# A gated mix of two attentions on one core: the first 512 tokens turned by TensorE instead of by DMA

## The chip, the cores and the metric

The kernel runs on one core of a Trainium2 chip. The metric is the device time of one execution in microseconds (us); for each kernel several executions are timed and the median is taken. One further execution is recorded by the hardware profiler, and all views below are of that one.

The core's engines are named as in the profile: PE is TensorE (matrix products), PEld its weight loads, DVE is VectorE, ACT is ScalarE, POOL is GpSimd, SP the engine that issues most DMAs.

## The reference

One input x of 2048 tokens by 512 goes through two attention blocks, each with 32 heads of 16, and the results are mixed by a gate per token:

```python
x = A_x
g = sigmoid((x * gate_w).sum(-1, keepdims=True))
# A: softmax attention
q, k, v = split(x @ A_wqkv)                     # 32 heads of 16
p = softmax(q @ k.T / 4)                        # 2048 x 2048 for each head
a = (p @ v) @ A_wo
# B: linear attention with a learned feature map
q, k, v = split(x @ B_wqkv)
phi = lambda t: concat(softmax(t @ w_phi), softmax(-(t @ w_phi)))
kv, z = phi(k).T @ v, phi(k).sum(tokens)
b = (phi(q) @ kv / (phi(q) @ z + 1e-6)) @ B_wo
return g * a + (1 - g) * b
```

Block A has 32 x 2048 x 2048 = 134 million exponentials; they are the bulk of the work.

## The kernel before, in words

**Tiles.** x is kept turned, as `xT` (features on the partitions, 4 chunks of 128, tokens along the row). From it `kT`, `qT` and `V` are projected. A *unit* is a score tile of one head: 128 keys by 512 queries, one bank of PSUM. Four units (four heads) of one key tile make a *pack*; a *head group* is 16 packs (all key tiles of four heads, for one chunk of 512 queries); there are 32 head groups and 512 packs.

**Two ways to take an exponential.** Most packs go to ScalarE: `_qk` writes three or two banks of scores (a ring of five banks), `_exp` reads them in one ACTIVATE and writes bf16 to slots of `ET` (30 slots), and `_pv` multiplies by V. The packs named in `AWAY` (a bit mask of up to five packs for each head group) go to VectorE instead: `_vector_bits` turns scores into bf16 bit patterns with one multiply-add, and `_vector_terms` (VectorE and GpSimd) makes two shifted copies whose sum corrects the approximation; TensorE adds the three terms. Block B's steps, the projections of later heads, and the stores are fitted in between.

**Order.** All work is declared as operations with an engine, an estimated cost, dependencies and a priority (a due time in packs). A planner (`Plan.order`) simulates five engines and writes an in-order queue for each; in the same sweep it hands out the free PSUM banks. Each operation belongs to a tag such as `p37` or `b103`, and the table `SHIFT` moves the priorities of a tag by a number found by search. The queues are fixed when the kernel is built.

**The start.** `_loads` queues on SP two transposing DMAs for the first 512 tokens (256 each, lines 529 to 531 and 1390), then three for the other tokens (512 each), then weights. ACT's own queue carries the first 128 columns of the key, query and value weights (`WA`, line 525). `_warm` (line 635) runs nine matmuls on ones from the start. `_proj_k0` and `_proj_q0` then project keys and queries of the first head group in halves of 256 tokens, each needing one of the two DMAs. The queries are copied out of PSUM twice, each time times a mask that keeps every other head (line 719, VectorE, four copies in all). The first scores need both halves of the queries and the first half of the keys.

Lines that the prediction names: 525 (loads of `WA`), 572 (ones for the warm-up), 639 (warm-up), 646 (projections in four column tiles), 662 (key projection in halves), 678 (its copy), 713 and 719 (query projection and its copies), 736 (value projection), 940 (`_vector_bits`), 1022 (scores), 1070 (exponentials), 1135 (products with V), 1238 (a copy of turned weights of block B out of PSUM), 1390 (transposing DMAs), 1496 (the last copies of the output by ScalarE), 1501 (stores).

Of the kernel before, what the change touches and what calls it, by code (L numbers as in the profile page):

```python
# [6 lines left out]
ACT = mybir.ActivationFunctionType  # L7
# [3 lines left out]
P = 128  # L11
# [375 lines left out]
class _Kernel:  # L387
# [122 lines left out]
    def _loads(self):  # L510
# [18 lines left out]
        for half in range(2):  # L529
            load_x(0, QCH // 2 * half, QCH // 2 * (half + 1), 4.1)  # L530
            self.b_x0[half].writers = self.b_xT[0].writers[half:]
# [64 lines left out]

    def _projections(self):
# [11 lines left out]
        self._warm(9)  # L609
# [25 lines left out]
    def _warm(self, n):  # L635

        def run(e):
            for _ in range(n):
                ins = e.matmul(self.ps[:, 4, :], self.warm[:, 0:P], self.warm, start=True, stop=True)
            return ins  # L640
        self.plan.op("PE", run, 0.427 * n, reads=[self.b_warm], name="warm", prio=-99)
# [63 lines left out]
    def _proj_q0(self, half, bank):  # L705
# [12 lines left out]
        for side in range(2):  # L718
            o = op("DVE", lambda e, side=side: e.tensor_scalar(
                self.qT[:, side, at], self._bank(job)[:, 0:QCH // 2], self.mask[:, side:side + 1], None, op0=ALU.mult),  # L720
                self.c_dve(256), reads=[self.b_mask], deps=[m], name="qproj_ev", prio=-40 + 70 * side,
                release=pool if side else None)
            self.b_qT[side].writers.append(o)
# [23 lines left out]
    def _gate(self):  # L747
# [44 lines left out]
    AWAY = (22, 27, 28, 19, 26, 15, 29, 27, 27, 15, 15, 30, 31, 13, 15, 27, 15, 23, 31, 27, 27, 31, 31, 31, 26, 31, 25, 31, 30, 15, 19, 31)  # L792

    SHIFT = (
# [752 lines left out]
```

## Time and profile before

| | us |
|---|---|
| median of 3 runs (lowest, highest) | 743.38 (743.01, 743.54) |
| the profiled execution, its own time | 743.37 |
| its span, first to last instruction | 741.6 |
| ACT busy in it | 727.0 |
| DVE busy in it | 693.9 |
| PE busy in it | 710.9 |

The granted TensorE clock is 1.00 over the whole span. How to read the views: a row of instructions gives its start and length in us, the engine, the line of the kernel, output and inputs by tile name, and in brackets how long the engine stood idle before and what ended that. A row of groups gives the number of instructions, their busy time, the mean length of one in ns, and the idle time before them. A row of stretches gives, after the stretch and its length, the busy time of PE, PEld, DVE, ACT and POOL with their numbers of instructions, then the granted clock, the share of the DMA engines and GB/s. A row such as "272/273/321" has the shortest, median and longest duration in ns. Lengths of instructions on one engine overlap, since the engines are pipelined.

### The profile page before, as it was taken

What the parts mean: (1) busy time and instruction counts of PE and PEld (TensorE: products, weight loads), DVE (VectorE), ACT (ScalarE), POOL (GpSimd) and SP (SyncE); (2) the same over time, 40 slices, a digit from 0 to 9 for tenths busy, and PEclk for the clock granted to TensorE, in tenths of its full rate; (3) what the DMA queues carried; (4) which work ended last, traced back from release to release, by engine and by line L of the source; (5) the groups of instructions that cost most, each with busy time, mean ns of one, the idle gap of its engine ahead of it and who ended that gap; (6) DMA issues with size and microseconds to landing.
All of it is one profiled execution on the core that took longest, in us unless ns stands there. A gap on an engine that the chain in (4) does not pass through costs nothing.

```text
span 741.6 us, 19810 instructions
## 1 busy us (share of the span) xinstructions
PE 710.9 (96%) x8580; PEld 232.8 (31%) x8599; DVE 693.9 (94%) x1097; ACT 727.0 (98%) x635; POOL 279.7 (38%) x277
## 2 busy tenths in 40 slices
PE   8999999999999999999998999999999999999998
PEld 4334333333232322322222223322323233322322
DVE  5889989988999999999999999999999999999996
ACT  6999999999999999999999999999999999999996
POOL 4631331423434335232434344245342433325342
PEclk9999999999999999999999999999999999999999
DMA  9400000000000010000101301131211320231110
GB/s 201 142 12 14 12 2 13 13 4 13 14 9 11 3 22 8 9 9 8 16 8 20 55 14 32 30 76 13 31 23 30 51 44 8 39 81 20 23 23 30
DMA packets 90040, 21.96 MB, mean 30 GB/s; under 512 B 82912, under 2 KB 89440, under 8 KB 89952
## 3 DMA queue, kind: packets, MB, share of 16 engines
q1 hardware_dynamic: 88224, 20.17, 14.5%
q8 instruction: 67, 1.10, 0.6%
q10 hardware_dynamic: 1728, 0.52, 0.3%
q14 instruction: 21, 0.17, 0.1%
HBM read 4.21 MB, written 2.10 MB: 9 GB/s over the span
## 4 chain that ended last, share of the span: by engine, by line
ACT 89%; PE 6%; DVE 2%; DMA 1%; SPq 0%; issue 0%; DVEq 0%
ACT ET L1070 85%; ACT bq L1308 4%; PE ps L1022 2%; PE ps L1135 2%; PE ps L646 2%; DVE va L940 1%; DVE vp L962 1%; DMA xT<-in_A_x_dram 1%; DMA WT<-nb 1%; PE ps L736 0%; DVE bq L1279 0%; DVE nb L1420 0%; SPq L1390 0%; ACT xT L1496 0%; DVE rb L1418 0%
## 5 line engine op out<-in xcount | busy, mean ns | idle before, releaser
L1070 ACT ACTIVATE ET<-ps 128x1536 bf16<-128x1536 f32 x615 | 699.8, 1372 | 5.2 <-PE ps L1022 4.9
L977 POOL TENSOR_SCALAR vp<-va 128x1024 uint16<-128x1024 uint16 x260 | 271.8, 1045 | 450.4 <-DVE va L940 137.7
L940 DVE TENSOR_SCALAR va<-ps 128x512 uint16<-128x512 f32 x512 | 335.2, 684 | 25.1 <-PE ps L1022 22.0
L1022 PE MATMUL ps<-qT,kT 32*128 32x512 bf16 x2048 | 311.6, 384 | 20.3 <-ACT ET L1070 15.9
L1022 PEld LDWEIGHTS ps<-qT,kT 32*128 32x128 bf16 x2048 | 81.0, 91 | 265.9 <-ACT ET L1070 165.3
L962 DVE TENSOR_SCALAR vp<-va 128x4096 uint16<-128x4096 uint16 (+1 forms) x143 | 159.4, 1123 | 0.6 <-PE ps L1135 0.4
L1135 PE MATMUL ps<-ET,V 128*32 128x512 bf16 x1536 | 148.4, 385 | 1.4 <-DVE T L1156 1.3
L1135 PE MATMUL ps<-vp,vc 128*32 128x512 bf16 x1024 | 93.3, 384 | 0.3 <-DVE vp L962 0.3
L646 PE MATMUL ps<-WB,xT 128*32 128x512 bf16 x768 | 57.9, 382 | 0.0
L1135 PEld LDWEIGHTS ps<-ET,V 128*32 128x32 bf16 x1536 | 39.3, 95 | 57.1 <-issue 40.7
L1142 PE MATMUL ps<-kT,zero 128*32 128x512 bf16 x552 | 50.1, 385 | 0.4 <-ACT ET L1070 0.3
L1135 PE MATMUL ps<-va,V 128*32 128x512 bf16 x512 | 50.2, 385 | 0.0
L1135 PE MATMUL ps<-vp,V 128*32 128x512 bf16 x512 | 47.1, 384 | 0.7 <-DVE vp L962 0.7
L646 PE MATMUL ps<-xT,WA 128*32 128x512 bf16 x480 | 36.1, 382 | 0.3 <-DVE va L940 0.3
L1135 PEld LDWEIGHTS ps<-vp,vc 128*32 128x32 bf16 x1024 | 24.4, 95 | 35.9 <-issue 24.9
L1308 ACT ACTIVATE bq<-bq 128x2048 bf16<-128x2048 bf16 x16 | 32.7, 2046 | 0.0
L1156 DVE STREAM_TRANSPOSE T<-ps 128x512 f32<-128x512 f32 x32 | 22.7, 709 | 1.7 <-PE ps L1135 1.7
L646 PE MATMUL ps<-WoA,onTA 128*32 128x512 bf16 x256 | 23.2, 383 | 0.0
L646 PE MATMUL ps<-WoB,WT 128*32 128x512 bf16 x256 | 23.0, 383 | 0.0
L1279 DVE CAST bq<-ps 128x512 bf16<-128x512 f32 x32 | 21.8, 683 | 1.1 <-PE ps L646 1.1
L646 PEld LDWEIGHTS ps<-WB,xT 128*32 128x32 bf16 x768 | 15.6, 95 | 19.0 <-issue 11.2
L1135 PEld LDWEIGHTS ps<-va,V 128*32 128x32 bf16 x512 | 13.3, 95 | 20.4 <-issue 16.6
(86 smaller groups left out, 357.9 us busy)
## 6 DMA issues: line engine op xcount, KB each, us to landing
turned<-T SPq DMA_DIRECT2D x240, 8.0 KB, 1.8
qT<-qs SPq DMA_DIRECT2D x120, 16.0 KB, 1.8
WB<-in_B_wqkv_dram SPq DMA_DIRECT2D x1, 1536.0 KB, 6.9
out_dram<-WB SPq DMA_DIRECT2D x12, 128.0 KB, 1.9
WA<-in_A_wqkv_dram SPq DMA_DIRECT2D x3, 384.0 KB, 6.1
WoA<-in_A_wo_dram SPq DMA_DIRECT2D x1, 512.0 KB, 7.9
WoB<-in_B_wo_dram SPq DMA_DIRECT2D x1, 512.0 KB, 8.8
WA<-in_A_wqkv_dram ACTq DMA_DIRECT2D x3, 128.0 KB, 3.6
```

What stands on the lines that cost most here:

```text
L646: ins = e.matmul(out[32 * g:32 * g + 32], lhs[:, 32 * g:32 * g + 32], rhs, start=start, stop=stop, tile_position=(0, 32 * g), skip_group_c ...
L940: parts.append(op("DVE", lambda e, j=j, job=job: e.tensor_scalar(self.va[:, pair, side, j, :], self._bank(job), SCALE * LOG2E * 128.0, (12 ...
L962: self.plan.op("DVE", lambda e, k=k, shift=shift: e.tensor_scalar(flat(self.vp[:, k]), flat(self.va[:, pair]), float(shift), None, op0=ALU ...
L977: o = self.plan.op("POOL", lambda e, flat=flat: e.tensor_scalar(flat[0], flat[1], 1.0, float(shift), op0=ALU.mult, op1=ALU.add), 0.08 + n ...
L1022: return e.matmul(out, self.kT[32 * i:32 * i + 32, cp, kt * TOK:(kt + 1) * TOK], self.qT[32 * i:32 * i + 32, s, :], start=True, stop=True, ...
L1070: o = plan.op("ACT", lambda e: e.activation(self.ET[:, a % NS:a % NS + n, :], self.ps[:, self._ring(a):self._ring(a) + n, :], ACT.Exp, sca ...
L1135: ins = e.matmul(self._bank(ot)[32 * i:32 * i + 32, :], V[:, v0:v0 + 32], tile(), start=(kt == 0), stop=(kt == self.NT - 1), tile_position ...
L1142: ins = e.matmul(self._bank(ot)[32 * i:32 * i + 32, :], self.zero[:], self.kT[:, 0, 0:QCH], start=False, stop=False, tile_position=(0, 32 ...
L1156: self.turned_out = op("DVE", lambda e: e.transpose(T1[:, side].rearrange("p b s -> p (b s)"), src()), 0.635, deps=last, writes=[b_T1[side ...
L1279: [lambda e, b, k=k: e.tensor_copy(bq[:, k].rearrange("p (g s v) -> p g s v", g=8, s=2)[:, :, 0, :], b.rearrange("p (g v) -> p g v", g=8))],
L1308: op("ACT", lambda e, side=side: e.activation(sides[side], sides[side], ACT.Exp, scale=1.0 - 2 * side), self.c_act(2048) + 0.04, reads=[bu ...
```

## The change

The first 512 tokens are loaded by four plain DMAs of 128 tokens each, as they lie, into slots 20 to 23 of `ET` (not yet used at that time). TensorE turns each with four transposes into one PSUM bank; the bank is copied to `xT` by VectorE for the first and third set of tokens, by ScalarE for the second and fourth. The nine warm-up matmuls become four, with one more after the second and one after the fourth set. Of the four masked copies of queries, one (second half, first mask) moves to ScalarE. `AWAY` and the whole table `SHIFT` are replaced; the table has 128 bits set before and after.

```diff
-        for half in range(2):
-            load_x(0, QCH // 2 * half, QCH // 2 * (half + 1), 4.1)
-            self.b_x0[half].writers = self.b_xT[0].writers[half:]
+        self.x0 = [self.dma("SP", f"x{t}", lambda e, t=t: e.dma_start(
+            self.ET[:, 20 + t], self.x2d[TOK * t:TOK * t + TOK, :]), cost=0.45, prio=-60 + t, lat=2.3) for t in range(4)]
...
+    def _first_tokens(self):
+
+        op = self.plan.op
+        for t in range(4):
+            job, pool = self._job(t if t < 2 else None)
+
+            def turn(e, t=t, job=job):
+                for c in range(4):
+                    ins = e.transpose(self._bank(job).bitcast(BF16)[:, P * c:P * c + P], self.ET[:, 20 + t, P * c:P * c + P], self.iden[:])
+                return ins
+            m = op("PE", turn, 4 * self.c_pe(128), reads=[self.b_iden], deps=[self.x0[t]], name="xtr", prio=-90 + t,
+                   acquire=pool)
+            if t % 2:
+                self._warm(1, [m])
+            out = self.xT[:, :, TOK * t:TOK * t + TOK]
+            src = lambda job=job: self._bank(job).bitcast(BF16)[:, 0:QCH].rearrange("p (c j) -> p c j", c=4)
+            if t % 2:
+                o = op("ACT", lambda e, out=out, src=src: e.activation(out, src(), ACT.Copy), self.c_act(QCH), deps=[m],
+                       name="xtr_ev", prio=-90 + t, release=pool)
+            else:
+                o = op("DVE", lambda e, out=out, src=src: e.tensor_copy(out, src()), self.c_dve(QCH), deps=[m],
+                       name="xtr_ev", prio=-90 + t, release=pool)
+            if pool is None:
+                self.early[t] = o
+            self.b_x0[t // 2].writers.append(o)
+        self.b_xT[0].writers = self.b_x0[0].writers + self.b_x0[1].writers
...
-        self._warm(9)
+        self._warm(4)
+        self._first_tokens()
...
-    def _warm(self, n):
+    def _warm(self, n, deps=()):
...
         for side in range(2):
-            o = op("DVE", lambda e, side=side: e.tensor_scalar(
-                self.qT[:, side, at], self._bank(job)[:, 0:QCH // 2], self.mask[:, side:side + 1], None, op0=ALU.mult),
-                self.c_dve(256), reads=[self.b_mask], deps=[m], name="qproj_ev", prio=-40 + 70 * side,
-                release=pool if side else None)
+            if half and not side:
+                o = a = op("ACT", lambda e: e.activation(
+                    self.qT[:, 0, at], self._bank(job)[:, 0:QCH // 2], ACT.Copy, scale=self.mask[:, 0:1]),
+                    self.c_act(256), reads=[self.b_mask], deps=[m], name="qproj_ev", prio=-40)
+            else:
+                o = op("DVE", lambda e, side=side: e.tensor_scalar(
+                    self.qT[:, side, at], self._bank(job)[:, 0:QCH // 2], self.mask[:, side:side + 1], None,
+                    op0=ALU.mult), self.c_dve(256), reads=[self.b_mask], deps=[m, a if half else None], name="qproj_ev",
+                    prio=-40 + 70 * side, release=pool if side else None)
...
-    AWAY = (22, 27, 28, 19, 26, 15, 29, 27, 27, 15, 15, 30, 31, 13, 15, 27, 15, 23, 31, 27, 27, 31, 31, 31, 26, 31, 25, 31, 30, 15, 19, 31)
+    AWAY = (29, 22, 22, 22, 7, 23, 23, 29, 15, 29, 29, 31, 7, 27, 27, 29, 31, 25, 31, 25, 31, 31, 27, 15, 30, 31, 15, 31, 28, 31, 23, 27)
...
```

The replaced table `SHIFT` is left out: several hundred pairs of a tag and a number, all of them other numbers than before.

More of the change, by code (lines that the diff above doesn't have):

```diff
@@ L640, in run @@
             return ins
-        self.plan.op("PE", run, 0.427 * n, reads=[self.b_warm], name="warm", prio=-99)
+        self.plan.op("PE", run, 0.427 * n, reads=[self.b_warm], deps=deps, name="warm", prio=-99)
     def _quarters(self, e, out, lhs, rhs, start, stop):
```

200 rows, old and new, of the table SHIFT are left out of this document.

## The prediction

> **What bounds the kernel now.** I read the page's engine shares first, then the chain that ended last, then the span cut at the start of the first exponential and at the end of the last one.
>
> ```profile
> PE 710.9 (96%) x8580; PEld 232.8 (31%) x8599; DVE 693.9 (94%) x1097; ACT 727.0 (98%) x635; POOL 279.7 (38%) x277
> ACT 89%; PE 6%; DVE 2%; DMA 1%; SPq 0%; issue 0%; DVEq 0%
> 0.00:8.32 8.32, 6.54 (x34) 3.26 (x35) 3.48 (x11) 1.29 (x2) 6.38 (x14) 1.00 0.90 182
> 8.32:733.43 725.11, 699.79 (x8468) 227.55 (x8489) 686.81 (x1080) 724.62 (x632) 273.28 (x263) 1.00 0.15 27
> 733.43:741.60 8.17, 4.55 (x88) 2.03 (x76) 3.57 (x7) 1.09 (x2) 0.00 (x0) 1.00 0.19 64
> ```
>
> Three engines are over 90% busy, but only one has no room. In the middle row ACT (the fourth busy figure) works 724.62 of 725.11 us: from its first exponential to its last it idles 0.49 us. So the time is three terms: 8.32 us until the first exponential, 725.11 us of ACT work, 8.17 us after the last one. The profiled execution took 743.37 us against a span of 741.60, so 1.77 us lie around the span; the median is 743.38, so sums against the profiled run can be read as sums against the median.
>
> ```profile
> L1070 ACT ACTIVATE ET<-ps 128x1536 bf16<-128x1536 f32 x307 | 486.2, 1584 | 5.2 <-PE ps L1022 4.9 <-PE ps L1135 0.2
> L1070 ACT ACTIVATE ET<-ps 128x1024 bf16<-128x1024 f32 x307 | 357.0, 1163 | 0.0
> L1496 ACT ACTIVATE xT<-ps 128x512 bf16<-128x512 f32 x2 | 1.1, 596 | 4.2 <-PE ps L646 4.2
> ```
>
> Does the change take work from ACT's middle term? No. Counting the set bits of AWAY gives 128 score packs for VectorE before and 128 after, hence 1536 banks and 615 exponentials (307 of three banks, 307 of two, one of one) in both. The split of the vector packs into 72 turns, 16 of them of one pack, is also the same. A new order can win at most the 0.49 us of idle there and can lose any amount. What can shrink is the head.
>
> ```profile
> 0.74 1.35 SPq L1390
> ...
> 2.14 4.49 DMA xT<-in_A_x_dram
> 6.63 0.04 issue
> 6.67 0.61 PE ps L713 x4
> 7.29 0.44 PE ps L662 x4
> 7.72 0.22 PE ps L736 x4
> 7.95 0.35 PE ps L1022 x3
> 8.29 0.02 issue
> 8.32 3.71 ACT ET L1070 x3
> ```
>
> This is the chain in order of time over the first 12 us. The second transposing load (tokens 256 to 511) is issued at 2.14 and lands at 6.63. Then come 0.61 of query projection, the masking copy on VectorE (the chain shows PE work of the same time instead), the scores, and the first exponential at 8.32: 1.69 us after the landing.
>
> **The change, part by part.**
>
> *The loads.* Two transposing DMAs go; four plain ones of 128 tokens (128 KB each, rows of 1 KB) come, all on SP's queue.
>
> ```profile
> 0.74 1.55 ACTq L525 DMA_DIRECT2D WA<-in_A_wqkv_dram  x3
> 10.90 1.68 SPq L525 DMA_DIRECT2D WA<-in_A_wqkv_dram  x3
> 738.10 1.31 SPq L1501 DMA_DIRECT2D out_dram<-xT  x3
> WA<-in_A_wqkv_dram ACTq DMA_DIRECT2D x3, 128.0 KB, 3.6
> out_dram<-xT SPq DMA_DIRECT2D x3, 128.0 KB, 1.9
> GB/s 0 0 0 0 0 46 229 260 288 290 287 249 192 207 194 158 280 276 178 219 283 289 240 200 72 111 260 271 289 263 177 179 230 127 277 290 278 218 268 334
> ```
>
> An issue on SP costs 0.44 (1.31/3) to 0.56 us (1.68/3); I take 0.50, so the fourth load is issued at 0.74 + 3 x 0.50 = 2.24. Its landing is not in this trace. From below: a store of the same size with the same rows lands 1.9 us after issue on quiet queues, so 4.14. From above: the first loads of WA on ACT's queue, also 128 KB but in short pieces and behind the transposes, have a median of 3.6, so 5.84; but x and WA together are 4 x 128 + 3 x 128 KB = 0.92 MB, and at the 290 GB/s that the last line reaches (40 slices of 0.35 us; first bytes near 1.9) all of it is in by 1.9 + 3.2 = 5.1. I take 4.5, nearer to the store, whose shape it has. The other three transposing loads move up in SP's queue: they follow 2.7 us into the span, so nothing that waits for later tokens is pushed back.
>
> [...]
>
> *Transposes and their copies.* Added: 16 PE transposes and four copies of 128x512 out of PSUM, the last one on ACT.
>
> ```profile
> 1.45 4.02 PE L639 MATMUL ps<-bq 128*128 128x512 bf16 x9 [1.45 <-DVE bq L572]
> 7.56 0.39 PE L736 MATMUL ps<-WA,xT 128*128 128x128 bf16 x4
> L639 PE MATMUL ps<-bq x9: 610/634/634, 1.5 to 4.8; 128*128 128x512 bf16 x9
> L662 PE MATMUL ps<-xT,WA x8: 272/273/321, 5.3 to 7.5; 128*128 128x256 bf16 x8
> L1022 PE MATMUL ps<-qT,kT x5: 384/384/385, 7.9 to 8.6; 32*128 32x512 bf16 x5
> 5.96 0.42 DVE L678 CAST kT<-ps 128x256 bf16<-128x256 f32 x1 [3.71 <-PE ps L662]
> 6.48 1.72 DVE L719 TENSOR_SCALAR qT<-ps,mask 128x256 bf16<-128x256 f32 x4
> L1238 DVE COPY WT<-ps x4: 628/664/692, 38.2 to 65.0; 128x1024 bf16<-128x1024 bf16 x4
> ```
>
> From the fourth landing on: four transposes of 128 columns 0.39 (the L736 row), ACT's copy 0.60 (the L1496 row), projection 0.61, ACT's copy of queries, scores 0.38, and five hand-overs of 0.04. ACT has no copy of 256 elements in the trace. From the copy of 512 (0.60) less 256 elements at the slope between the two exponentials ((1584 - 1163)/512 = 0.82 ns) it is 0.39; VectorE's masked copy, 1.72/4 = 0.43 apart, is the other end; I take 0.43. Sum: 0.39 + 0.60 + 0.61 + 0.43 + 0.38 + 0.20 = 2.61. Key and query projections of the first half (about 0.44 each, the 7.29 row) may also stand between the last transposes and the query projection on PE; ACT's copy hides 0.60 of these 0.88, and I add 0.25. So 2.86 after the landing, against 1.69 before: the turning costs 1.17 us, the earlier landing gives 6.63 - 4.5 = 2.13.
>
> **First exponential: 4.5 + 2.86 = 7.36, which is 0.96 us earlier.**
>
> At no cost: VectorE's two copies (under 0.66 each, the L1238 row for twice the elements), since it stands idle 3.71 us before its first cast; ACT's three copies, since they lie before the first exponential, where ACT waits 4.71 of its 5.2 us; one exponential-table load is already there and L1496 copies under it. The five warm-up matmuls removed cost nothing if the array's clock has risen anyway (below). Added waits: the PE instructions behind the fourth transpose set wait for a load; that wait is in the 4.5.
>
> *The new order.* Same work, other places. I take 0 for it, with -0.4 and +3.5 as ends.
>
> ```profile
> 177.51 16.02 ACT L1070 ACTIVATE ET<-ps 128x1536 bf16<-128x1536 f32 x14 [0.16 <-PE ps L1135]
> 537.45 15.48 ACT L1070 ACTIVATE ET<-ps 128x1536 bf16<-128x1536 f32 x13 [0.23 <-PE ps L1022]
> ```
>
> These are the only two waits of ACT in the middle, 0.16 and 0.23 us. VectorE has 725.11 - 686.81 = 38.3 us of slack and PE 25.3 us, 1.2 and 0.8 us per 22.7 us head group, so a bad place can hit; the upper end is 16 such waits (one in every second head group) at 0.22 us. The tail, 8.17 us, is a fixed series of one normalization, one projection and the stores; I leave it, within 0.3.
>
> Forecast: 743.38 - 0.96 = **742.4 us**.
>
> **Rivals.**
>
> *The loads land early (741.6).* All as above, but the fourth load lands at its lower bound, 4.14 or a little under (0.44 per issue: 3.96), and the two first-half projections fit wholly under ACT's copy: 3.96 + 2.61 = 6.57, a gain of 1.75. For: same shape as the store. Against: 0.92 MB want the queues together.
>
> *The loads are late, or ACT takes a second table load (743.0).* At the byte bound of 5.1 the gain is 0.36. If the copy that now comes first on ACT brought a table load of its own ahead of that for the exponentials, the head would lose most of its gain too; against it, the trace shows copies and exponentials under one load.
>
> *TensorE stays slow (745.1, slower).* The nine warm-up matmuls of 512 columns follow each other every (4.02 - 0.63)/8 = 0.42 us and last 634 ns; the first projection at 5.27 already has 273 ns for 256 columns, and the 512-column scores 384. So the array doubled its rate after some 3.8 us of dense work. With four, the dense stretch ends at 1.45 + 4 x 0.42 = 3.1; then come transposes as loads land, with gaps, and two single warm-ups. If the rate hasn't doubled when the fourth load lands, PE has, one after another: four transposes 0.42, a warm-up 0.42, projections of four times 0.21 three times over (2.5), and 0.2 of drain: 4.5 + 3.5 = 8.0; with copy 0.43, scores 0.63 and hand-overs 9.2, so 0.9 later than before. Until the rate doubles PE then lags further, and PE has no idle time in this stretch; with 0 to 1.6 us of that reaching ACT the time is 744.3 to 745.9. Point of decision: the length of the first 256-column projection, 273 ns or about 420.
>
> [...]
>
> *The new order costs more (744.9).* Twelve waits of 0.2 us on ACT and the head's gain: 742.4 + 2.4. For: VectorE and PE are near full throughout, every place is new. Against: 615 exponentials now run with two waits, and no dependency is added past the head.
>
> **How the numbers follow.** A measurement of this kernel can tell about 0.2%, 1.5 us: faster is under 741.9, slower over 744.9. Forecast 0.46 (its own range 741.8 to 743.1), early 0.18, late 0.06, slow TensorE 0.15, worse order 0.15. Faster: early and the lowest part of the forecast, 0.18 + 0.08 = 0.26. Slower: two thirds of the last two, 0.20. Same: 0.54. The range takes in all but the ends of the early case (0.07) and of the last two (0.12): 741.3 to 745.5.
>
> **What would show it.** Right: a first exponential at 7.0 to 7.8; the four x loads in by 4.3 to 5.0; ACT idle under 1 us after it; one table load; 273 ns projections. Wrong: any 420 ns projection, ACT waits summing to over 1 us between first and last exponential, or a first exponential past 8.

## The result and the profile after

| | before | changed |
|---|---|---|
| median (lowest, highest) of 6 runs each, us | 743.06 (742.88, 743.54) | 746.76 (745.98, 747.15) |
| profiled execution, its own time | 743.37 | 746.55 |
| its span | 741.6 | 744.8 |

The changed kernel is slower: ratio 1.0042, 95% interval 1.0031 to 1.0052, some 3 us by the ratio and 3.70 by the two medians. That is clear of the noise, though under half a per cent. The forecast was 742.4 in a range of 741.3 to 745.5.

The engine shares, and the engine shares of the chain that ended last, of the changed kernel:

```profile
PE 713.5 (96%) x8629; PEld 233.4 (31%) x8640; DVE 694.8 (93%) x1098; ACT 728.4 (98%) x638; POOL 279.4 (38%) x277
ACT 69%; PE 21%; DVE 6%; SPq 2%; DMA 1%; issue 1%
```

The same three stretches as in the prediction, cut at the first exponential and at the end of the last (columns as there):

```profile
0.00:11.48 11.48, 9.23 (x47) 5.12 (x48) 4.08 (x12) 2.95 (x4) 6.38 (x14) 1.00 0.91 198
11.48:737.14 725.66, 701.46 (x8540) 227.29 (x8549) 687.17 (x1080) 724.32 (x632) 273.00 (x263) 1.00 0.14 26
737.14:744.80 7.66, 2.79 (x48) 0.98 (x44) 3.57 (x7) 1.09 (x2) 0.00 (x0) 1.00 0.21 68
```

The head grew from 8.32 to 11.48 (+3.16), the middle from 725.11 to 725.66 (+0.55), the tail shrank from 8.17 to 7.66 (-0.51). Together +3.20, the difference of the two spans. The +0.55 is no more than single executions differ by: in the five profiled executions that keep the old order in its own program (the kernel before and four runs below) the middle measures 723.81 to 725.68. The chain's engine shares have moved from ACT to PE, but the middle row says that ACT still works 724.32 of 725.66 us there: a chain that runs through PE is no loss as long as ACT does not wait. The loss is in the first 12 us, and there the chain reads, in order of time:

```profile
2.12 4.11 DMA ET<-in_A_x_dram
6.23 0.05 issue
6.28 0.61 PE ps L604 x4
6.89 0.43 PE ps L666
7.31 0.85 PE ps L689 x4
8.17 1.71 PE ps L740 x8
9.87 0.85 PE ps L689 x4
10.73 0.39 PE ps L768 x4
11.11 0.32 PE ps L1054 x3
```

Two things stand out. The fourth load lands at 6.23, not at 4.5 (it takes 4.11 us). And from there PE is the chain for 5.2 us, while before 1.69 us passed between the landing and the first exponential. L604 are the transposes, L666 the warm-up, L689 and L740 the key and query projections, L768 value projections, L1054 the first scores. The durations of the transposes and of the query projections in ns, shortest, median and longest:

```profile
L604 PE MATMUL ps<-iden,ET x16: 266/314/314, 3.3 to 6.6; 128*128 128x128 bf16 x16
L740 PE MATMUL ps<-xT,WA x8: 421/421/421, 8.0 to 9.5; 128*128 128x256 bf16 x8
```

The same query projections in the kernel before, and three rows of PE in the changed kernel:

```profile
L713 PE MATMUL ps<-xT,WA x8: 272/272/283, 5.8 to 7.0; 128*128 128x256 bf16 x8
```

```profile
5.34 0.61 PE L604 MATMUL ps<-iden,ET 128*128 128x128 bf16 x4
7.11 1.06 PE L689 MATMUL ps<-xT,WA 128*128 128x256 bf16 x4
7.96 1.91 PE L740 MATMUL ps<-xT,WA 128*128 128x256 bf16 x8
```

A projection of 256 columns takes 421 ns; before it took 272 at this place. As these lengths overlap, the rate is better read from the distance between two starts: 0.21 us now ((1.91 - 0.42)/7), 0.11 before ((0.61 - 0.27)/3, from the 0.61 of four in the chain of the kernel before). So TensorE's array runs at half rate, up to about 10.7, although the granted clock in the stretch reads 1.00: that column does not show this.

ACT's own rows show that the last query copy is ready at 9.91 + 0.47 = 10.38, but the scores it was made for start at 11.05 and the exponential at 11.48, since PE runs its queue in order and the second key projection and four value-projection matmuls stand ahead:

```profile
9.91 0.47 ACT L747 ACTIVATE qT<-ps,mask 128x256 bf16<-128x256 f32 x1 [2.39 <-PE ps L740]
11.48 4.62 ACT L1102 ACTIVATE ET<-ps 128x1536 bf16<-128x1536 f32 x4 [1.10 <-PE ps L1054]
```

### The profile page after: what moved, and what is told of

It is laid out like the page before. It is cut to its first block, busy times and chain, and to the rows that moved or that the text cites. A ratio compares the mean times of both kernels' runs of the same rounds, so it can differ in the third digit from the quotient of the medians.

```text
span 744.8 us, 19930 instructions
## 1 busy us (share of the span) xinstructions
PE 713.5 (96%) x8629; PEld 233.4 (31%) x8640; DVE 694.8 (93%) x1098; ACT 728.4 (98%) x638; POOL 279.4 (38%) x277
## 4 chain that ended last, share of the span: by engine, by line
ACT 69%; PE 21%; DVE 6%; SPq 2%; DMA 1%; issue 1%
ACT ET L1102 66%; PE ps L1054 7%; PE ps L1167 7%; PE ps L673 4%; ACT bq L1340 3%; DVE va L972 2%; DVE vp L994 1%; PE ps L1174 1%; PE ps L768 1%; SPq L1422 1%; SPq L726 1%; DMA ET<-in_A_x_dram 1%; DMA WT<-nb 1%; DVE T L1188 0%; DVE nb L1452 0%
## 5 line engine op out<-in xcount | busy, mean ns | idle before, releaser
L1054 PE MATMUL ps<-qT,kT 32*128 32x512 bf16 x2048 | 308.1, 384 | 15.7 <-ACT ET L1102 11.4
L1054 PEld LDWEIGHTS ps<-qT,kT 32*128 32x128 bf16 x2048 | 81.1, 91 | 262.5 <-ACT ET L1102 157.8
L1174 PE MATMUL ps<-kT,zero 128*32 128x512 bf16 x592 | 54.0, 385 | 0.0
L1174 PEld LDWEIGHTS ps<-kT,zero 128*32 128x32 bf16 x592 | 13.7, 94 | 23.4 <-issue 21.7
```

Source lines behind the costliest of these rows:

```text
L1054: return e.matmul(out, self.kT[32 * i:32 * i + 32, cp, kt * TOK:(kt + 1) * TOK], self.qT[32 * i:32 * i + 32, s, :], start=True, stop=True, ...
L1174: ins = e.matmul(self._bank(ot)[32 * i:32 * i + 32, :], self.zero[:], self.kT[:, 0, 0:QCH], start=False, stop=False, tile_position=(0, 32 ...
```

## The experiments

Theory A: the loss is the array's half rate at the start, since four warm-ups and transposes with gaps no longer wake it. Theory B: it is the late landing of x. Theory C: it is the new order. Each ratio below is to the kernel before as measured beside that run, and each trace is of one execution. In all runs of parts, unless said otherwise, the queues are those that the planner wrote for the unchanged parent; the edits are made inside an operation or on the finished queues.

**Array kept busy.** One more warm-up matmul behind the first and the third set of transposes:

```diff
                     ins = e.transpose(...)
+                for _ in range((1, 0, 1, 0)[t]):
+                    e.matmul(self.ps[:, 4, :], self.warm[:, 0:P], self.warm, start=True, stop=True)
                 return ins
```

> The changed kernel, its order untouched, with one more 512-column warm-up matmul run behind the transposes of the first and of the third set of tokens, so that PE has nearly no gap from 1.45 us to the fourth landing. Theory A (the array's clock had not risen): the first key projection takes 273 ns for 256 columns instead of 421, the first exponential starts at about 9.2 instead of 11.5, the time is about 744.5 (-2.3). [...] Theory B (the late fourth load, landing at 6.23, is the whole loss): PE's rate does not matter, 746.5 or more. Theory C (the new order): 746.8.

Measured 744.27 (743.85 to 745.83), ratio to before 1.0018, interval 1.0009 to 1.0027, wholly under that of the changed kernel. PE's rows:

```profile
4.42 0.63 PE L668 MATMUL ps<-bq 128*128 128x512 bf16 x1
5.64 0.40 PE L604 MATMUL ps<-iden,ET 128*128 128x128 bf16 x4 [0.59 <-DMA ET<-in_A_x_dram]
6.42 0.40 PE L604 MATMUL ps<-iden,ET 128*128 128x128 bf16 x4 [0.17 <-DMA ET<-in_A_x_dram]
6.87 0.60 PE L691 MATMUL ps<-xT,WA 128*128 128x256 bf16 x4
```

The third set of transposes takes 0.40 us where it took 0.61, and four projections 0.60 where they took 1.06: the rate has doubled by 5.64. ACT starts at 9.43:

```profile
9.43 4.62 ACT L1104 ACTIVATE ET<-ps 128x1536 bf16<-128x1536 f32 x4 [0.58 <-PE ps L1056]
```

The fourth load of x, in the chain, lands at 6.37:

```profile
2.12 4.25 DMA ET<-in_A_x_dram
```

So two matmuls more take 2.05 us off the head, though x lands no earlier (6.37 against 6.23). This is Theory A, for about two thirds of the head's 3.16 us. The remaining 1.1 us are not.

**Plain matmuls instead of transposes,** with the same two fillers: `e.matmul(bank, ET chunk, iden)` for `e.transpose`, the copies reading fp32.

> As warm_fill, but the 16 transposes are plain matmuls against the identity into fp32 PSUM, of the same 128 columns (VectorE's two copies then read fp32: about 0.68 instead of 0.42 us). If transposes do not count as activity of the array and plain matmuls do, this one rises early (273 ns, first exponential about 9.2, 744.5) and warm_fill does not. If both count, the two are within 0.5 us of each other. Theory B and C: 746.8, as the changed kernel.

Measured 744.73 (744.29 to 746.44), ratio 1.0025, interval 1.0014 to 1.0035, within 0.5 us of the run with transposes as expected if both count. In its profiled execution, which at 745.84 is one of the longer ones of this run, the rate rose only at about 9.4:

```profile
5.79 0.61 PE L604 MATMUL ps<-iden,ET 128*128 128x128 bf16 x4 [0.65 <-DMA ET<-in_A_x_dram]
7.47 1.06 PE L691 MATMUL ps<-xT,WA 128*128 128x256 bf16 x4
9.72 0.60 PE L691 MATMUL ps<-xT,WA 128*128 128x256 bf16 x4
```

Plain matmuls did no better than transposes, so this gives no support to the case in which only they count. But one execution, in which the third set of transposes started 0.15 us later than in the other kernel, does not settle it; the transposed warm-up below says more.

**Four warm-ups in the kernel before,** nothing else changed (`range(4)` in place of `range(n)` in `_warm`).

> The kernel before, its order untouched, with four warm-up matmuls run instead of nine. Theory A: without the dense stretch the first projections at 5.1 us run at half rate here too (421 ns), the first exponential moves from 8.3 to about 9.5 to 10.5, the time to about 744.5 to 745.5 with no other part of the change in it. Theory B and C: 743.1, as before.

Measured 744.97 (743.61 to 745.7), ratio 1.0018, interval 1.0008 to 1.0028: the removed warm-ups alone, with no other part of the change, make the kernel slower. PE and ACT:

```profile
1.45 1.89 PE L639 MATMUL ps<-bq 128*128 128x512 bf16 x4 [1.45 <-DVE bq L572]
5.29 1.03 PE L662 MATMUL ps<-xT,WA 128*128 128x256 bf16 x4 [1.95 <-DMA xT<-in_A_x_dram]
6.12 1.91 PE L713 MATMUL ps<-xT,WA 128*128 128x256 bf16 x8
9.24 0.61 PE L1022 MATMUL ps<-qT,kT 32*128 32x512 bf16 x3
```

```profile
9.90 2.37 ACT L1070 ACTIVATE ET<-ps 128x1536 bf16<-128x1536 f32 x2 [6.30 <-PE ps L1022]
```

PE stands still for 1.95 us before the first load, projections then run at half rate (1.91 us for eight), and the first exponential comes at 9.90 instead of 8.32.

**Later loads held back.** In the changed kernel, the first transposing load (tokens 512 on) waits on SP for the fourth plain load:

```diff
             p.order()
+            late = [o for o in p.ops if o.name == f"dma_x{QCH}"]
+            late[0].deps.append(self.x0[3])
```

> The changed kernel, its order untouched, but the first transposing load (tokens 512 to 1023) waits on SP until the fourth plain load has landed. Theory B with contention (the transposing load's 256-byte packets take the DMA engines from the fourth load): the fourth load lands at about 5.3 instead of 6.23, the first exponential moves up by up to 0.9 us to 10.6, the time to 746.0 unless later keys come too late. Without contention: it lands at 6.2 as it did, and the later tokens come 3.6 us later, 746.8 or more. Theory A alone: 421 ns stays.

Measured 745.62 (744.02 to 746.53), ratio 1.0025, interval 1.0015 to 1.0035, which overlaps the changed kernel's. The fourth set is turned at 6.10 instead of 6.28:

```profile
6.10 0.61 PE L606 MATMUL ps<-iden,ET 128*128 128x128 bf16 x4 [0.23 <-DMA ET<-in_A_x_dram]
```

So the transposing load behind it costs the fourth load at most about 0.2 us, not 0.9 (with unchanged queues the landing differed by 0.14 between the changed kernel and the run with fillers). The run "Value weights after x" below takes out another load. The nine times of this run fall in two groups, 744.02 to 744.36 and 745.62 to 746.53; only one execution, of the longer group, was profiled, and why the others are shorter is not shown.

**The order tables alone, both ways.** The kernel before with the new `AWAY` and `SHIFT`, and the changed kernel with the old ones; here the planner runs anew on the pairing.

> The kernel before with only the new AWAY and SHIFT tables: nine warm-ups, transposing loads, all query copies on VectorE. Theory A (the loss is the start alone: slow clock and late loads): the first exponential stays near 8.3, the stretch from it to the last one near 725.4 and the tail near 7.6, as they are in the changed kernel, so 742.5 to 743.5. Theory C (the new order costs the rest): 744.5 or more, with ACT waits over 1 us after the first exponential.

> The changed kernel with the old AWAY and SHIFT tables. Theory A: the first exponential comes at 10.9 to 11.6 as in the changed kernel, the time is 746 to 747.5. Theory C: a first exponential at 11 but a total under 745, since the order's cost is gone.

Measured 799.96 (798.0 to 804.46), ratio 1.0767 (1.0728 to 1.0807), and 806.91 (804.13 to 810.37), ratio 1.0867 (1.0826 to 1.0909). Theory A's forecasts missed by more than 50 us in both; Theory C's "744.5 or more" takes the first in only because it has no upper end, and its "under 745" for the second missed too. ACT's waits in the two, by what ended them (total, times, longest):

```profile
ACT ET L1070 <- PE ps L1022: 26.8, 25, 7.9
ACT ET L1070 <- PE ps L1135: 24.8, 9, 10.2
```

```profile
ACT ET L1102 <- PE ps L1167: 41.9, 12, 14.0
ACT ET L1102 <- PE ps L1054: 8.4, 14, 1.5
```

In these two pairings a table is of no use to a program that it was not searched for: ACT waits some 50 us, in single waits of up to 14. (The granted clock averages 0.973 and 0.981 in these two; what that adds is not separated here.) The new search was therefore a condition of the change, not an extra; the two runs say nothing on which table is better. For that there are only the middle and the tail. With the new order the middle measures 725.21 to 725.66 in seven profiled executions, with the old one 723.81 to 725.68 in five; the tail measures 7.57 to 7.66 against 8.12 to 8.18. So the new order has a tail shorter by about 0.5 us; its middle is longer by 0.95 in the median (725.45 against 724.50), which with such a spread is not settled.

**Warm-up by transposes.** The kernel before with 36 transposes of 128 columns in place of nine matmuls of 512.

> The kernel before with its nine 512-column warm-up matmuls replaced by 36 transposes of 128 columns, the same 4608 columns at the same time (they wait for the identity, 0.1 us later). If transposes count as activity of the array: the first key projection takes 273 ns, the first exponential comes at 8.3 to 8.5, 743.3. If they do not: 421 ns until some 9 to 12 us, first exponential at 9.9 or later as with four warm-ups, 745 to 746.

Measured 742.76 (741.94 to 743.29), ratio 0.9989, interval 0.9980 to 0.9998. PE's first rows, the durations of the query projections, and ACT's first exponential:

```profile
1.62 4.00 PE L640 MATMUL ps<-iden,bq 128*128 128x128 bf16 x36 [1.62 <-POOL iden L558]
5.42 1.06 PE L663 MATMUL ps<-xT,WA 128*128 128x256 bf16 x4
```

```profile
L714 PE MATMUL ps<-xT,WA x8: 272/273/417, 6.3 to 7.2; 128*128 128x256 bf16 x8
```

```profile
8.92 31.75 ACT L1071 ACTIVATE ET<-ps 128x1536 bf16<-128x1536 f32 x28 [5.31 <-PE ps L1023]
```

The rate doubles at the second of the query projections, about 6.5, when plain matmuls had run for 1.1 us only. With four warm-ups it took projections from 5.29 to beyond 9.24. So the transposes counted. Whether they count in full is open: neither leg of the expectation came as written, since the first key projection is still at half rate (1.06 us for four) and the first exponential starts at 8.92, not at 8.3 to 8.5; with nine matmuls it rose earlier, between 5.3 and 5.9: in three executions the four key projections that start at 5.27 took 0.65, 0.72 and 0.93 us (0.60 at full rate). The time of 742.76 does not speak for the start either: in the profiled execution the head is 0.60 longer than that of the kernel before and the middle, which the edit does not touch, 1.30 shorter (723.81).

**Value weights after x.** The changed kernel with the two fillers, and the load of the first value weights behind the x loads:

```diff
             p.order()
+            act, sp = p.queues["ACT"], p.queues["SP"]
+            w = next(o for o in act if o.name == "dma_wa20")
+            act.remove(w)
+            sp.insert(1 + next(i for i, o in enumerate(sp) if o.name == "dma_x3"), w)
```

> The changed kernel with the two extra warm-up matmuls of warm_fill, and the load of the first 128 columns of the value weights moved from ACT's queue to SP's, behind the fourth x load. The queue view says that the seven loads of 128 KB take turns at about 0.55 us each, so one less ahead of it brings the fourth x load in at about 5.7 instead of 6.4, and the first exponential from 9.4 to about 8.7: 743.5. If the loads of x are paced by something else, it stays at 6.3 and 744.3.

Measured 743.89 (743.48 to 744.94), ratio 1.0009, interval 1.0000 to 1.0019. The fourth set is turned at 5.86, 0.56 us earlier than with the fillers alone, and ACT starts 0.57 us earlier:

```profile
5.86 0.39 PE L608 MATMUL ps<-iden,ET 128*128 128x128 bf16 x4
```

```profile
8.86 4.62 ACT L1108 ACTIVATE ET<-ps 128x1536 bf16<-128x1536 f32 x4 [0.58 <-PE ps L1060]
```

One 128 KB load less in the queues brings the last x in sooner: the fourth load lands 3.5 us after its issue at 2.12, so at about 5.6 instead of 6.37, and its set then stands behind other work on PE until 5.86. The 0.56 us of the turning reaches the first exponential in full. The intervals of the two times overlap (1.0009 to 1.0027 and 1.0000 to 1.0019). This shows what an earlier landing is worth; it is no part of what the change did, as both kernels load these weights ahead of x's last part.

**Attempts at a faster version.** First the changed kernel: `fill_wv_late` with the last warm-up cut to 16 columns, the fourth copy on VectorE, the first scores ahead of the value projection; then the same with two x loads of 256 tokens.

> fill_wv_late with three more moves at the start: the warm-up behind the fourth set of tokens is cut to 16 columns, the fourth copy goes from ACT (0.60 us) to VectorE (0.42), and the first scores stand ahead of the first four value-projection matmuls on PE instead of behind them. Counting from the rows of fill_wv_late: key projection from 6.1 instead of 6.3, query projections done at 7.55 instead of 7.75, scores 0.2 sooner after the copy: first exponential at about 8.45 instead of 8.86, time 743.0 to 743.5, level with the kernel before. If the clock rises later without that warm-up, 744 or more.

> As tuned, but the four x loads are two of 256 tokens (256 KB each). If the landing of x is paced by a fixed cost per load that does not overlap (seven loads taking turns), all of x is in at 5.2 to 5.4 instead of 5.7 and the first exponential at about 8.1: 742.9. If it is paced by bytes and packets alone, x is in at 5.7 as before, the first set is turned later, and the time is that of tuned or up to 0.3 more.

Measured 743.75 (743.48 to 746.39), ratio 1.0014 (1.0006 to 1.0022), and 744.37 (743.51 to 745.32), ratio 1.0020 (1.0011 to 1.0028): neither is faster than `fill_wv_late`. First exponentials:

```profile
8.94 4.62 ACT L1119 ACTIVATE ET<-ps 128x1536 bf16<-128x1536 f32 x4 [0.58 <-PE ps L1071]
```

```profile
9.14 4.63 ACT L1129 ACTIVATE ET<-ps 128x1536 bf16<-128x1536 f32 x4 [0.58 <-PE ps L1081]
```

In the first, x came in earlier still (the fourth load at about 5.4), but the rate rose only during the projections at 6.19 (0.78 us for four, 0.60 at full rate), which took the gain back. In the second, PE's rows at the first and the third set:

```profile
3.83 0.58 PE L628 MATMUL ps<-iden,ET 128*128 128x128 bf16 x4 [0.49 <-POOL V L590]
5.49 0.63 PE L628 MATMUL ps<-iden,ET 128*128 128x128 bf16 x4
```

The larger loads do land sooner: the second was issued at 1.2 and took 3.7 us, so all of x was in at about 4.9, half a microsecond before the four loads. But the first landed later (at about 3.7, while the row names an instruction of GpSimd that ended at the same time), so the first set was turned 0.7 us later, and from then on PE was busy without a gap at half rate (0.63 us for four transposes, 0.39 at full rate), transposes and fillers in turn. The last set was turned at 6.32, long after it had landed. So this run does not say that larger loads are of no use, only that behind these fillers they are not.

Then the kernel before, with the value weights behind its second transposing load:

> The kernel before with one edit: the load of the first 128 columns of the value weights goes from ACT's queue to SP's, behind the second transposing load. If the loads at the start take turns, the second half of x lands at about 6.1 instead of 6.63, the first exponential starts at about 7.9 instead of 8.3 and the time is 742.8 to 743.1; if the transposing loads pace themselves, or the value weights then come too late (after 7.5), nothing or a loss of up to 0.5.

Measured 742.59 (742.14 to 743.59), ratio 0.9997 (0.9989 to 1.0006): nothing. The second half of x is in a microsecond earlier, at 5.67 (issued at 2.15, landed after 3.5), but a wait takes the place of the one removed, on PE, for the value weights:

```profile
7.50 0.40 PE L740 MATMUL ps<-WA,xT 128*128 128x128 bf16 x4 [0.20 <-DMA WA<-in_A_wqkv_dram]
```

This run has a second use. With the value weights out of the way in both kernels, the transposing loads have the first 512 tokens in at 5.67 here, already turned; the plain loads have them in at about 5.6 in `fill_wv_late` (5.4 in the first attempt above), still to be turned. In this comparison the plain loads, the reason for the change, gain 0.1 to 0.3 us, not the 2.13 of the forecast.

Last, the same with the first scores ahead of those matmuls and VectorE's copies in the order of need:

```diff
+            k = next(o for o in pe if o.name == "qk0")
+            pe.remove(k)
+            pe.insert(next(i for i, o in enumerate(pe) if o.name == "vproj"), k)
+            s = [o for o in dve if o.name == "qproj_ev"][1]
+            k1 = [o for o in dve if o.name == "kproj_ev"][1]
+            dve.remove(s)
+            dve.remove(k1)
+            at = 1 + [i for i, o in enumerate(dve) if o.name == "qproj_ev"][1]
+            dve[at:at] = [k1, s]
```

> before_wv_late with the two waits taken out that stood behind the earlier landing (5.67 instead of 6.63): the first scores go ahead of the first four value-projection matmuls on PE (these waited until 7.50 for the value weights), and on VectorE the second mask's copy of the first query half goes behind the first mask's copy of the second half and the key copy. Then the query projection ends at 6.87, its copy at about 7.35, the scores at 7.75: first exponential at 7.8 instead of 8.3, 0.5 us less than the kernel before and 4 us less than the changed one: 742.3. If the second exponential then waits for the later copies (0.3 or more), 742.6 to 742.8.

Measured 742.12 (741.77 to 743.42) against 743.12, ratio 0.9987, interval 0.9978 to 0.9996: the lowest of all, 0.13% under the kernel before. Its start:

```profile
5.27 0.93 PE L676 MATMUL ps<-xT,WA 128*128 128x256 bf16 x4
7.68 0.39 PE L1036 MATMUL ps<-qT,kT 32*128 32x512 bf16 x3 [0.17 <-DVE qT L733]
```

```profile
8.12 31.84 ACT L1084 ACTIVATE ET<-ps 128x1536 bf16<-128x1536 f32 x28 [5.07 <-PE ps L1036]
```

The first exponential came at 8.12, not 7.8: in this execution the rate rose late in the first key projections, four of which took 0.93 us instead of 0.65. So the head is 0.20 us shorter than that of the kernel before. The rest of the microsecond between the medians is not in the start: the run before this one has the same span (740.8) with a head of 8.31, and the transposed warm-up measured 0.9989 with a longer head. Ratios of this size are not settled by these runs.

## Why the prediction was wrong, point by point

The three terms and the place of the loss were right; two entries of the sum for the head failed. The removed warm-ups, put at nothing, cost about 2.2 us through the array's rate, and the landing, put at 4.5, came 1.73 us later.

- *What bounds the kernel, and the three terms.* Right. ACT's middle stretch and the tail changed by +0.55 and -0.51, and the head decided. That the two cancel is luck in part: the tail was to stay within 0.3.
- *First exponential: 7.36.* Failed: 11.48, so 4.12 us off. By the next steps 1.73 of these are the landing (6.23 for 4.5), and 2.39 the way from there to the first exponential (5.25 for 2.86).
- *The new order at 0, within -0.4 and +3.5.* Right in size, as far as a middle that varies between executions can show it. That the table cannot be carried to another program at all was not foreseen.
- *Landing of the fourth load: 4.5, at most 5.1.* Failed: 6.23. Of the loads at the start the trace after shows (last row: the first 14 us in 40 slices of 0.35)

```profile
ET<-in_A_x_dram SPq DMA_DIRECT2D x4, 128.0 KB, 3.3
WA<-in_A_wqkv_dram ACTq DMA_DIRECT2D x3, 128.0 KB, 3.4
GB/s 0 0 0 0 0 102 155 293 330 337 275 244 207 255 269 242 234 203 290 290 289 142 179 138 230 184 287 290 256 206 167 181 282 287 289 73 167 184 316 366
```

  x took 3.3 us in the median and 4.11 for the fourth load, not 1.9 like a store on quiet queues. And the upper bound was none: it put a rate of 290 GB/s in for the whole time, where the thirteen slices from 1.75 to 6.3 us have a mean of 242, the transposing load behind x included. Leaving that load out was the smaller fault: with it held back the seven loads, 0.92 MB, still took from 1.75 to 6.05, a mean of 213 GB/s. Taking one of the seven out moved the landing by some 0.7 us (6.37 to about 5.6), holding the transposing load back by 0.2.
- *From the landing to the first exponential: 2.86.* With the array at full rate this was nearly right: 9.43 - 6.37 = 3.06 in the run with fillers. At half rate it was 5.25. So of the 2.39 us above 0.20 are the sum's own (it leaves out the warm-up behind the fourth set, 0.22 in that run's chain), and 2.19 the array's rate.
- *The five warm-ups at no cost.* This step failed worst. The condition was stated ("if the array's clock has risen anyway"), but the term was put at nothing, and the rival in which the condition fails was given 0.15. Fillers alone win 2.05 us of the head back, and taking the warm-ups out of the kernel before costs 1.58 us of its head with nothing else changed.
- *The rival of a slow TensorE, 745.1.* Its mechanism, its place and its sign (421 ns, as named) were right. Of what it lists behind the four warm-ups the gaps hold and the transposes do not: with the same 16 transposes and two fillers the rate had risen by 5.64 (0.40 us for four transposes instead of 0.61). From the landing it counted 3.5 us of serial PE work; the rows give 6.28 to 9.87. Its first exponential of 9.2 became 11.48 by the landing (+1.7) and by scores that stand behind a key projection and four value matmuls (0.67 us after the copy).
- *Second table load, order waits.* The one table load stays. ACT's idle in the middle is 1.34 us (0.49 before), over the 1 us that was named as a sign of being wrong, but far from the 2.4 of that rival; ACT's busy time there fell by 0.30, so the middle grew by 0.55 only.
- *After how much work the rate rises.* The rival took some 3.8 us of dense work from one trace. With dense work from 1.45 us on the rate rose 3.8 to 4.5 us later in three executions with nine matmuls (0.65, 0.72 and 0.93 us for four projections at 5.27); with four and a gap of 1.95 us it was still at half at 9.24 (0.61 us for three scores, 0.39 at full rate). Weighing this rival higher than 0.15 would have saved the sign. Transposes in place of the matmuls counted as well: after 36 of them the rate rose with 1.1 us of plain matmuls, though somewhat later (about 6.5) than after nine matmuls (5.3 to 5.9).

The head's +3.16 us can be added up from the rows: the earlier landing gives 0.40 (6.63 to 6.23), the way from the landing to the first exponential costs 1.37 more at full rate (3.06 against 1.69), since x is still to be turned and copied, and the half rate costs 2.19 (5.25 against 3.06). The last term is shown both ways, by the fillers and by the four warm-ups in the kernel before. The 1.37 are read from one execution of each kernel, and no run parts them further. The change needed an early landing to pay for the turning, and that did not come.

## What to carry to other kernels

A warm-up is work with a job: before removing part of it, add up how long TensorE would then stand idle until the first real matmul, and price everything up to the first output at half rate (here, with four warm-ups in the kernel before, 1.95 us of idle and then 421 ns instead of 272 for each projection). A bound on a landing must count all transfers issued around it at the rate that the trace shows on average, and not at its peak (here 242 GB/s, where the bound put 290). And a wait that is taken away at the start of an in-order queue can be worth nothing while another stands behind it: a landing 0.96 us earlier moved the first exponential by 0.01 us in one run; with the first scores and copies moved ahead as well it came 0.20 earlier.

## What the runs showed of the hardware that was not expected

- The array's rate did not rise at a fixed time after the first matmul. With the same nine warm-ups from 1.45 us on, four 256-column projections at 5.3 us took 0.65 us in the kernel before and 0.93 in the last run: in one execution it had risen, in the other it rose in their midst. How much of the spread of times comes from this is not shown, as one execution of each run was profiled.
- Transposes counted towards the array's rate: after 36 of them it doubled at about 6.5, while with four warm-up matmuls and a gap it was still at half at 9.24.
- Why the kernel with transposes as warm-up measured 0.9989 of the kernel before stays open; its profiled head is 0.60 us longer, and its middle 1.30 shorter.
